# One written order for four engines in a dilated convolution kernel

## The chip, the cores and the metric

The kernel runs on one core of one Trainium2 chip. The metric is the device time of one execution in microseconds. Three runs of the kernel before took 267.48, 267.99 and 269.68 us; their median is 267.99 us. A profile was taken of one further execution.

## The reference

The input x has 2 sequences of 16000 time steps with 256 channels, in bf16. A causal convolution with three taps and dilation 2 gives 512 channels; one half goes through tanh, the other through a sigmoid, their product is multiplied with a 256 x 256 matrix:

```python
B, T, D, K = (2, 16000, 256, 3)
dil = 2
pad = (K - 1) * dil
xp = jnp.pad(x, ((0, 0), (pad, 0), (0, 0)))
h = jnp.einsum('btc,cd->btd', xp[:, pad:pad + T, :], w[0])
for i in range(1, K):
    off = pad - i * dil
    h = h + jnp.einsum('btc,cd->btd', xp[:, off:off + T, :], w[i])
f = h[..., :D].copy()
g = h[..., D:].copy()
z = jnp.tanh(f) * _sigmoid(g)
return z @ w_o
```

## The kernel before

**Groups and blocks.** Time is cut into 26 groups of rows, a row being 4 or 6 successive time steps. A group of kind B (13 of them, 4 steps a row) computes two outputs of each parity from four products where the direct way needs six; a group of kind A (12, 6 steps a row) computes three outputs from five products where the direct way needs nine. One small group P at the very start is done directly. A group has R = 256 rows (160 in the last one and in P), loaded transposed by one DMA on SyncE's queue (line 286). Each A or B group has four blocks, one for every 128 of the 512 channels: 100 blocks in all. The list `seq` holds them in order: four B groups, then A and B blocks mixed, then two B groups.

**What a block needs.** Its products are two matmuls each (two halves of the 256 input channels), 2R columns wide. The letters are those of the code:

- F ("first") starts PSUM bank b. ScalarE copies it to SBUF (c, `copy_first`, line 484), since more is added to b later.
- M ("mid", kind A alone) adds to b. VectorE makes hh from the copy and b (h, `halfway`).
- L ("last") adds to b. VectorE then makes bank a from the copy and b (a) and, for kind A, a third result yy from hh and b (y); both stand in `combine`, and all of h, a and y are recorded at line 487.
- Z ("zero") adds to b, and I ("inf") adds to a. The block's outputs are in b, a and yy.
- ScalarE applies tanh or sigmoid to b, yy and a (b, y, a in its order; line 527). VectorE multiplies tanh and sigmoid halves (g, `gate`, line 547) after the second and the fourth block of a group.
- P: a piece of the last matrix product, four matmuls of 256 columns (`out_mm`, line 565). ScalarE evicts it (e, line 592; the last few go to VectorE at line 576, v), and a store on SyncE's queue follows when all pieces of 128 rows are evicted.

**Input sums.** The moving operands of the products are sums and differences of the loaded rows. VectorE makes most (`pre`, lines 432 and 434). GpSimd makes the operands d0 and d3 of most B groups and r0 and ri of the A groups, in quarters (lines 434). Two more, rm and rp, are made by accumulating DMAs on GpSimd's queue (line 429). GpSimd also adds up the weight matrix of F for the A groups in 16 pieces (wa.0 to wa.15). Each of GpSimd's sums is made to wait (`hold`) for a chosen instruction of VectorE, so that it starts beside one that reads PSUM.

**Slots.** The main loop goes through slots k = 0, 1, ...; in slot k, block k does F (and M), block k-1 does L and its combine, block k-2 does Z and I, and block k-3 has its last activation and its gate. TensorE's order in a slot is fixed by the kinds of the blocks k and k-1:

```python
PE_ORDER = {"AB": "FLZIM12", "AA": "FZLIM12", "BA": "FZLI12", "BB": "FZLI12", "": "LZI123"}
```

The digits are the pieces P, one or two per slot by a rule on the number waiting. ScalarE's order follows from this loop: activation a, one eviction, then copies and activations as their products are issued. On VectorE the gate, then a, y and h follow each other; a written plan (`PLAN`, one line per stop, taken at each gate, each combine and some evictions) tells which input sums VectorE makes before that instruction and which sums GpSimd is given there. Each engine executes its instructions in the order in which the loop issues them; the semaphores between engines are derived from what each one reads and writes.

**Buffers that matter.** Bank b has 3 buffers, so F of block k waits for the activation of b of block k-3. Bank a has 2, the output pieces have 3, the copies 3.

Of the kernel before, what the change touches and what calls it, by code (L numbers as in the profile page):

```python
# [13 lines left out]
PLAN = """  # L14
>m.0 p.0 d3.0 d0.0;
>d3.1;wa.2
>m.1;
>;wa.1
>p.1 d0.2 m.2;wa.5' wa.7
>d0.1;  # L20
>;wa.0
>e.0 u1.0;wa.10
>p.2;
>;wa.8 wa.9
>d3.2 f.0;wa.6' wa.13'
>m.3;
>ud.0;wa.4' wa.12
>uh.0 u0.0 u0.1;r0.0''
>u2.0;
>u3.0;ri.0'  # L30
>u2.1 d0.3;wa.14' wa.3
>d3.3;
>p.3;rp.0 r0.0'
>p.4 f.1;wa.11'
>u0.2;
>u1.1;rm.0 r0.0'
>d0.4 m.4;ri.0' d0.5'
>u1.2;
>d3.4;r0.0'
>ud.1 uh.2 e.1 uh.1;rp.1 r0.2' wa.15  # L40
>;
>u3.1;r0.2' ri.0 ri.0
>m.5 u3.2;d3.5'
>f.2 e.2;rm.1 ri.1' r0.1 r0.1'
>;
>;r0.2 r0.1
>;
>u1.3;ri.1' d0.5'
>u2.2 ud.2;d0.5' r0.1
>;  # L50
>;ri.1 d3.5 ri.1 ri.2 d3.5
>e.3;
>p.5 u3.3 f.3;rm.2 ri.2' d3.5'
>ud.3;
>;rp.2 r0.2
>;
>uh.3;d0.5' d3.6'
>u1.4 u3.4;rp.3 d0.6 d0.6'' ri.2' d3.6''
>u0.3;ri.2
>;  # L60
>u2.3;r0.3' d3.6
>f.4 uh.4;rm.3 ri.3' r0.3''
>;
>u0.4;ri.3' d0.6
>;
>e.4;r0.3' r0.3
>ud.4 m.6;d0.6' r0.4'
>p.6 e.5;ri.3' ri.3''
>;
>;d3.6 r0.4  # L70
>;
>u1.5;rm.4 d3.7'
>u2.4 uh.5 m.7;r0.4' ri.4''
>;
>;rp.4 d3.7 r0.4
>e.6 u3.5 ud.5;ri.4' ri.4
>u0.5 f.5;r0.5' ri.4''
>;
>;r0.5 d3.7
>;  # L80
>u1.6;rp.5 d0.7
>p.7 u2.5;rm.5 d3.7'
>ud.6;
>uh.6;ri.5' r0.5'
>u3.6 u0.6;ri.5' d0.7'
>f.6 u2.6;rm.6 r0.6'' ri.5 r0.5 d0.7
>;
>;ri.5
>;
>f.7;rp.6 d0.7' r0.6'  # L90
>u1.7;ri.6' r0.6'
>u0.7 u2.7;ri.6' ri.6
>;
>u3.7;r0.6' ri.6
>m.8 ud.7 e.7;d0.8' d3.8''
>u1.8;
>;rm.7 d3.8
>;
>;ri.7 d0.8 d0.8 ri.7
>p.8;d0.8'  # L100
>e.8 u3.8 u0.8;rp.7 ri.7' d3.8''
>uh.7;
>;r0.7 d0.9 r0.7 d3.8
>;
>;ri.7
>f.8 u2.8;d3.9' d0.9''
>;
>;r0.7 r0.7
>uh.8 e.9 ud.8;rm.8 ri.8''
>u1.9 uh.9;rp.8 d3.9 ri.8''  # L110
>;
>ud.9;ri.8'
>f.9;
>u3.9;ri.8' r0.8 r0.8
>u2.9;ri.9' r0.8'
>u0.9;d0.9 r0.8
>m.9;
>;d3.9 d3.10
>u1.10;rm.9 r0.9
>;  # L120
>p.9;rp.9 r0.9' d3.9'
>;
>uh.10;d0.9' d0.10'
>f.10 e.10;r0.9 ri.9''
>u3.10 u1.11;d0.10 ri.9''
>;
>;r0.9 ri.9
>;
>u2.10;rm.10 d0.10' d3.10
>u3.11 u0.10 ud.10;rp.10 ri.10'  # L130
>;
>;r0.10 ri.10 r0.10
>ud.11 p.10;r0.10' r0.10''
>e.11 m.10;d3.11' d3.11''
>;
>;ri.10 d3.10 ri.10
>;
>;d0.10 d0.11
>f.11 uh.11 u2.11;rm.11 d3.10 d3.12'
>u0.11;  # L140
>;rp.11 ri.11 r0.11 d3.12 ri.11
>;ri.11 ri.11
>;r0.11 r0.11
>m.11;
>;r0.11 d0.11
>;
>;
>;d3.11 d0.12 d3.12 d0.12
>;d0.12
>;  # L150
>;d0.11
>m.12 p.11;d3.11' d0.11
>;
>;d3.12
>;
>;
>;
>;
>;
p.12>;d0.12  # L160
>;
>;
>;
>;
>;
>;
>;
>;
>;
>;  # L170
>;
>;
# [4 lines left out]
def kernel(  # L177
# [10 lines left out]
    nc = tc.nc  # L188
    bf16 = mybir.dt.bfloat16
    f32 = mybir.dt.float32  # L190
# [15 lines left out]
    SOME, SOME_A = 5, 99  # L206
# [7 lines left out]
    def group(kind, b, t, R):  # L214
        of_kind[kind].append(len(groups))
        groups.append(dict(kind=kind, b=b, t0=t, R=R, J=ROWS[kind]))
        return t + ROWS[kind] * R

    for b in range(B):
        t = 0  # L220
        if b == 0:
            t = group("P", b, 0, 160)
        n_a, n_b = N_A[b], (T - t - 6 * RG * N_A[b]) // (4 * RG)
# [5 lines left out]
        if T > t:  # L229
            t = group("B", b, t, (T - t) // 4)  # L230
# [11 lines left out]
    SHARE = N - 3  # L242
# [254 lines left out]
    def combine(blk):  # L497


        at_stop()  # L500
        g, oi = blk
        G = groups[g]
        n = 2 * G["R"]
        b, ss = G["b", oi][:, :n], G["ss", oi][:, :n]
        G["a", oi] = ps_a.tile([P, 2 * RG], f32, name="a")
        stt(G["a", oi][:, :n], ss, 3.0 if G["kind"] == "A" else -2.0, b)
        if G["kind"] == "A":
            G["y", oi] = ss_pool.tile([P, 2 * RG], f32, name="yy")
            stt(G["y", oi][:, :n], G["hh", oi][:, :n], 2.0, b)
# [23 lines left out]
    def gate(g, dt):  # L533
        at_stop()
# [35 lines left out]
    def out_evict(g, rb0, jp, on_v=False):  # L570
# [3 lines left out]
        if on_v:  # L574
            at_stop()
# [13 lines left out]
        if jp == 0:  # L589
# [3 lines left out]
        if jp == J // 2 - 1:  # L593
# [10 lines left out]
    kinds = {n: groups[g]["kind"] for n, (g, _) in enumerate(seq)}  # L604
    stops = iter([[part.split() for part in re.split("[>;]", line)] for line in PLAN.strip().split("\n")])
    stop = next(stops)
# [68 lines left out]
    gate(0, 0)  # L675
    ahead()
# [5 lines left out]
    final = final[-1:] + final[:-1]  # L682

    todo, made, last_odd = [], [], []
    k = 0
    while k < N + 3 or todo or made:
        b0, b1, b2, b3 = (seq[n] if 0 <= n < N else None for n in (k, k - 1, k - 2, k - 3))
        kind = groups[b0[0]]["kind"] if b0 else None
        n = 1 + (len(todo) >= SOME_A) if kind == "A" else (k >= N + 3) + (not b0 or len(todo) >= SOME) + 1
        pieces = []  # L690
        while todo and todo[0][0] <= k and len(pieces) < n:
            pieces.append(todo.pop(0)[1])

        if b3:
            activate(b3, "a")
        for piece in made[:1]:
            out_evict(*piece)
        for what in PE_ORDER[(kind or "") + (kinds.get(k - 1, "B") if kind else "")]:
            if what == "F":
                product(b0, "first")  # L700
                copy_first(b0)
                if k == 0:
                    direct(3, TAPS[:2], (1,))
                if b2 and groups[b2[0]]["kind"] == "A":
                    activate(b2, "y")
            elif what == "M":
                product(b0, "mid")
            elif what == "L" and b1:
                product(b1, "last")
                if k == 1:  # L710
                    direct(3, TAPS[2:], (1,))
                    activate((0, 3), "a")
            elif what == "Z" and b2:
                product(b2, "zero")
                activate(b2, "b")
                for piece in made[1:] if k < SHARE else ():
                    out_evict(*piece)
            elif what == "I" and b2:
                product(b2, "inf")
            elif what in "123" and len(pieces) >= int(what):  # L720
                if k >= N + 3:
                    out_mm(*pieces[int(what) - 1], dts=(1,))
                elif k >= N and what == "2":
                    out_mm(*pieces[1], pool=ps_b, tag="b")
                else:
                    out_mm(*pieces[int(what) - 1])
        if k == N + 2:

            assert not todo
            for piece, (pool, tag) in zip(final, ((ps_a, "a"), (ps_b, "b"), (ps_o, "o_ps"))):  # L730
                out_mm(*piece, dts=(0,), pool=pool, tag=tag)
        if not b2 and k < SHARE:
            for piece in made[1:]:
                out_evict(*piece)

        if b3 and b3[1] in (1, 3):
            g, dt = b3[0], b3[1] // 2
            gate(g, dt)
            if dt == 1:
                todo += [(k + 1, piece) for piece in (final if g == seq[-1][0] else pieces_of(g))]  # L740
        if k == 0:
            weights_a(1 + K)
        if b1:
            combine(b1)
        if k == 1:
            gate(0, 1)
            todo += [(k + 1, piece) for piece in pieces_of(0)]
        if b0 and kind == "A":
            halfway(b0)
        for n, piece in enumerate(made[1:] if k >= SHARE else ()):  # L750
            out_evict(*piece, on_v=n == 0)
        ahead()
        made = pieces
# [4 lines left out]
        k += 1  # L758

    nc.scalar.dma_start(**last_odd[0])  # L760
# [30 lines left out]
```

## Time and profile before

| | |
|---|---|
| median of the three runs | 267.99 us |
| the profiled execution's own time | 267.66 us |
| its span, first to last instruction | 265.8 us |
| busy: TensorE / ScalarE / VectorE / GpSimd | 259.5 / 245.9 / 240.0 / 144.2 us |
| granted TensorE clock, mean | 0.995 |

Times in the profile are microseconds from the span's start. PE is TensorE's matmuls and PEld its weight loads, DVE is VectorE, ACT is ScalarE, POOL is GpSimd, SP is SyncE. A busy time counts a matmul from its start until its modelled end, which lies after the next one's start, so a short stall can hide in it. In rows of the timeline a trailing x2 means that two instructions of one kind were merged into one row, and a bracket gives the idle time before the row and what ended it. In the chain, each row is a start, a duration and what held the end of the program back at that time.

### The profile page before, as it was taken

How to read it: one execution, taken by the hardware profiler on the slowest of the kernel's cores; microseconds unless marked ns; L12 is line 12 of the kernel's file. 1: busy time of each engine (PE TensorE's matmuls, PEld its weight loads, DVE VectorE, ACT ScalarE, POOL GpSimd, SP SyncE). 2: the span in 40 equal slices, each digit the busy share in tenths (PEclk: the TensorE clock that was granted, in tenths of full speed). 3: DMA queues.
4: the chain of work that ended last, by engine and by line, in shares of the span. 5: the costliest groups of instructions: out<-in, count | busy, mean ns of one | idle time of the engine just before them, and what ended most of it. 6: DMA issues, size and time to landing. Idle time of an engine off the chain costs nothing.

```text
span 265.8 us, 4535 instructions
## 1 busy us (share of the span) xinstructions
PE 259.5 (98%) x1476; PEld 143.0 (54%) x1476; DVE 240.0 (90%) x396; ACT 245.9 (92%) x487; POOL 144.2 (54%) x209
## 2 busy tenths in 40 slices
PE   8999999999999999999999999999999999999993
PEld 4654555554555555555455555555555555555682
DVE  2999999999999999999999999999999996877472
ACT  5889999898999999999999999999999999999983
POOL 1034476677876666466755866476465677423000
PEclk9999999999999999999999999999999999999998
DMA  7999999569394589469729794796139464121225
GB/s 188 224 207 227 229 162 217 149 128 197 66 242 130 121 200 203 120 154 233 178 98 211 174 190 104 184 207 139 61 121 166 123 149 118 61 77 60 101 99 187
DMA packets 79583, 41.25 MB, mean 155 GB/s; under 512 B 68648, under 2 KB 69928, under 8 KB 79560
## 3 DMA queue, kind: packets, MB, share of 16 engines
q1 hardware_dynamic: 75060, 33.66, 52.4%
q0 software_dynamic: 3456, 6.29, 13.8%
q10 hardware_dynamic: 1044, 1.02, 1.2%
q8 instruction: 11, 0.18, 0.3%
q14 instruction: 12, 0.10, 0.1%
HBM read 1.25 MB, written 16.38 MB: 66 GB/s over the span
## 4 chain that ended last, share of the span: by engine, by line
PE 87%; DMA 3%; ACT 3%; DVE 3%; SPq 1%; issue 1%; DVEq 0%
PE b L453 52%; PE o_ps L565 20%; PE a L453 15%; DMA xt<-in_x_dram 2%; DMA w_sb<-in_w_dram 1%; ACT th L527 1%; ACT ss L484 1%; DVE a L487 1%; SPq L286 1%; DVE yy L487 1%; ACT sg L527 1%; DVE hh L487 1%; ACT osb L592 0%; DVE zz L547 0%; DVE p L434 0%
## 5 line engine op out<-in xcount | busy, mean ns | idle before, releaser
L487 DVE SCALAR_TENSOR_TENSOR a<-ss,b 128x512 f32<-128x512 f32 (+1 forms) x100 | 68.4, 684 | 10.3 <-PE b L453 9.3
L592 ACT CAST osb<-o_ps 128x512 bf16<-128x512 f32 x118 | 70.9, 601 | 4.7 <-PE o_ps L565 4.6
L565 PE MATMUL o_ps<-wo_sb,zz 128*128 128x256 bf16 x496 | 69.9, 273 | 0.0
L453 PEld LDWEIGHTS <-w_sb 128*128 128x128 bf16 x400 | 38.8, 97 | 47.2 <-issue 1.9
L484 ACT COPY ss<-b 128x512 f32<-128x512 f32 (+1 forms) x100 | 60.2, 602 | 2.9 <-ACT osb L592 0.8
L565 PEld LDWEIGHTS <-zz 128*128 128x128 bf16 x496 | 48.5, 98 | 25.3
L434 POOL TENSOR_TENSOR d<-xt 128x256 bf16<-128x256 bf16 (+1 forms) x64 | 41.9, 663 | 35.2 <-DVE zz L547 11.3
L434 POOL TENSOR_TENSOR u<-u,uh 128x256 bf16<-128x256 bf16 x48 | 37.6, 789 | 24.9 <-DVE zz L547 17.3
L434 POOL TENSOR_TENSOR u<-u,ud 128x256 bf16<-128x256 bf16 x48 | 36.9, 775 | 24.5 <-DVE zz L547 12.9
L547 DVE TENSOR_TENSOR zz<-th,sg 128x1024 bf16<-128x1024 bf16 (+2 forms) x52 | 41.4, 796 | 2.1 <-ACT sg L527 2.1
L487 DVE SCALAR_TENSOR_TENSOR hh<-ss,b 128x512 f32<-128x512 f32 x48 | 32.9, 684 | 2.7 <-PE b L453 2.2
L487 DVE SCALAR_TENSOR_TENSOR yy<-hh,b 128x512 f32<-128x512 f32 x48 | 32.7, 681 | 0.0
L453 PEld LDWEIGHTS <-wp_sb 128*128 128x128 bf16 x200 | 19.5, 97 | 24.4 <-issue 3.4
L527 ACT ACTIVATE th<-a 128x512 bf16<-128x512 f32 (+1 forms) x50 | 30.7, 614 | 2.0 <-PE a L453 1.0
L527 ACT ACTIVATE sg<-a 128x512 bf16<-128x512 f32 (+1 forms) x50 | 31.0, 619 | 1.5 <-PE a L453 0.4
L527 ACT ACTIVATE th<-b 128x512 bf16<-128x512 f32 (+1 forms) x50 | 30.7, 614 | 0.7 <-PE b L453 0.7
L527 ACT ACTIVATE sg<-b 128x512 bf16<-128x512 f32 (+1 forms) x50 | 30.7, 615 | 0.3 <-PE b L453 0.3
L453 PE MATMUL b<-d,w_sb 128*128 128x512 bf16 (+1 forms) x104 | 30.3, 373 | 0.2 <-DVE a L487 0.2
L453 PE MATMUL a<-d,w_sb 128*128 128x512 bf16 (+1 forms) x104 | 30.3, 373 | 0.0
L453 PE MATMUL b<-m,wm_sb 128*128 128x512 bf16 (+1 forms) x104 | 30.3, 373 | 0.0
L453 PE MATMUL b<-p,wp_sb 128*128 128x512 bf16 (+1 forms) x104 | 30.3, 373 | 0.0
L453 PE MATMUL b<-u,w_sb 128*128 128x512 bf16 x96 | 28.6, 379 | 0.5 <-DVE yy L487 0.3
(57 smaller groups left out, 330.0 us busy)
## 6 DMA issues: line engine op xcount, KB each, us to landing
out_dram<-osb SPq DMA_DIRECT2D x24, 384.0 KB, 2.7
out_dram<-osb SPq DMA_DIRECT2D x26, 256.0 KB, 2.6
f<-u POOLq DMA_DIRECT2D x12, 256.0 KB, 3.9
e<-u POOLq DMA_DIRECT2D x12, 256.0 KB, 3.6
w_sb<-in_w_dram ACTq DMA_DIRECT2D x3, 256.0 KB, 4.0
xt<-in_x_dram SPq DMA_TRANSPOSE x25, 5.4
xn<-in_x_dram SPq DMA_DIRECT2D x1, 160.0 KB
xn<-in_x_dram ACTq DMA_DIRECT2D x1, 160.0 KB, 4.4
```

What stands on the lines that cost most here:

```text
L286: ins = nc.sync.dma_start_transpose(out=xt[:, :, :, RH - lo:RH + R].rearrange("p j ct r -> p (j ct) r"), in_=x[G["b"], G["t0"] - J * lo:G[ ...
L434: ins = eng.tensor_tensor(out=o, in0=a, in1=b, op=op)
L453: nc.tensor.matmul(G[bank, oi][:, :2 * R], lhsT=wmat[:, ct, osl], rhs=G[mv][:, :, ct, :R], start=which == "first" and ct == 0, stop=ct == ...
L484: nc.scalar.copy(out=G["ss", oi][:, :n], in_=G["b", oi][:, :n])
L487: return note(nc.vector.scalar_tensor_tensor(out=out, in0=in0, scalar=scalar, in1=in1, op0=ALU.mult, op1=op))
L527: nc.scalar.activation(out=G[name, dt][:, j:j + 2, :R], in_=G[bank, oi][:, :2 * R].rearrange("p (q r) -> p q r", q=2), func=(ACT.Tanh, ACT ...
L547: note(nc.vector.tensor_tensor(out=G["z"][:, dt, :, :n], in0=G["th", dt][:, :, :n], in1=G["sg", dt][:, :, :n], op=ALU.mult))
L565: nc.tensor.matmul(o_ps[:, q, :], lhsT=z, rhs=wo_sb[:, dt, :], start=dt == 0 and (q == 0 or len(dts) == NT), stop=dt == NT - 1, skip_group ...
L592: copy(out=osb[:, 2 * jp:2 * jp + 2, :], in_=o_ps[:])
```

## The change

The plan has one line for each slot now, 106 lines with k = -1 first, and each line has four parts: TensorE's products and pieces in their order, ScalarE's activations, copies and evictions in theirs, VectorE's sums, gates, combines, halfways and evictions in theirs, and GpSimd's sums. The fixed table of orders, the rule on the number of pieces and the stops are gone. `combine` is split, so that a and y can stand apart (y may come before a). The instructions are the same in number and kind on each engine; which groups there are, how they load, and how far ahead, stays as it was. In code, the parts of a line are issued so that ScalarE's next letter goes out as soon as what it reads has been issued. GpSimd's sums are given out ahead of a in each slot.

```diff
 PLAN = """
->m.0 p.0 d3.0 d0.0;
->d3.1;wa.2
->m.1;
...
->f.2 e.2;rm.1 ri.1' r0.1 r0.1'
->;
->;r0.2 r0.1
...
+ |  | d3.0 m.0 p.0 d0.0 G | 
+F D D | c w |  | 
+F L D | c d | d3.1 a m.1 G | wa.7' wa.4
+F L Z I | c b | a | wa.1 wa.5
+L P F Z I | a c b | d0.2 a | wa.2
+L Z P F I | a b c | m.2 p.1 g a | wa.9
...
+F L I Z M P P | c a y b | e.2 a u3.1 h | ri.1' d0.5'
+F Z L I M | a e e c b | g f.2 a h y | rm.1 r0.1' r0.1 r0.2'
+F P I L Z P | a e c e y b | g u1.3 a y | ri.1' r0.2 ri.1'
+L F I Z M | a c y b | a u2.2 h | d0.5
+Z F L I M | a e c b | g a y h | r0.1 r0.2
...
+Z I P p P | a b | v | 
+H H H | a e E | g v | 
+R R R |  |  | 
+ | e E | v | 
 """
...
-    def combine(blk):
-
-
-        at_stop()
+    def combine(blk, what):
...
-        G["a", oi] = ps_a.tile([P, 2 * RG], f32, name="a")
-        stt(G["a", oi][:, :n], ss, 3.0 if G["kind"] == "A" else -2.0, b)
-        if G["kind"] == "A":
+        if what == "a":
+            G["a", oi] = ps_a.tile([P, 2 * RG], f32, name="a")
+            stt(G["a", oi][:, :n], ss, 3.0 if G["kind"] == "A" else -2.0, b)
+        else:
             G["y", oi] = ss_pool.tile([P, 2 * RG], f32, name="yy")
             stt(G["y", oi][:, :n], G["hh", oi][:, :n], 2.0, b)
...
-    def ahead():
-        sums(stop[0])
-        stop[0] = []
-
-    def at_stop():
-        nonlocal stop
-        sums(stop[1])
-        gpsimd(stop[2])
-        stop = next(stops, [[], [], []])
...
-    PE_ORDER = {"AB": "FLZIM12", "AA": "FZLIM12", "BA": "FZLI12", "BB": "FZLI12", "": "LZI123"}
...
-        n = 1 + (len(todo) >= SOME_A) if kind == "A" else (k >= N + 3) + (not b0 or len(todo) >= SOME) + 1
...
+    for k, line in enumerate(PLAN.strip().split("\n"), -1):
+        pe, act, dve, pool = (part.split() for part in line.split("|"))
         b0, b1, b2, b3 = (seq[n] if 0 <= n < N else None for n in (k, k - 1, k - 2, k - 3))
...
+        def scalar():
+
+            while waiting:
+                what = waiting[0]
+                there = {"c": "F" in done, "b": "Z" in done, "e": made, "E": made[1:], "d": not leftover}
+                if not there.get(what, True):
+                    break
+                waiting.pop(0)
+                if what == "c":
+                    copy_first(b0)
+                elif what in "by":
+                    activate(b2, what)
+                elif what == "a":
+                    activate(b3, "a")
...
+        scalar()
+        for what in pe:
+            if what in "FM":
+                product(b0, {"F": "first", "M": "mid"}[what])
+            elif what == "L":
                 product(b1, "last")
...
+            done.add(what)
+            scalar()
...
+        for what in dve:
+            if what == "g":
+                gate(b3[0], b3[1] // 2)
...
+            elif what == "a":
+                gpsimd(pool)
+                combine(b1, "a")
+            elif what == "y":
+                combine(b1, "y")
+            elif what == "h":
+                halfway(b0)
+            elif what == "v":
+                out_evict(*made.pop(0), on_v=True)
+            else:
+                sums((what,))
```

More of the change, by code (lines that the diff above doesn't have):

```diff
@@ new lines @@
+F I Z L P P | a y b c | y a g | r0.11
+F L I Z M | a c e y b | a h g | d3.11 d3.11 d3.11
+Z P F I L M | b c a e e | p.11 a h y | d3.12'
+F P P P I L Z P P | a e e c y b | m.11 a y | d3.11'
+L F I Z M | a y c b e | m.12 a h g | d0.11
+I Z F L P | a b c e | a y | d3.12 d0.11
+F L I Z | a c y b e | a g |
+L Z I F P | b a e c | p.12 a g | d0.12 d3.12
+F P P Z L I P | a e c e b e | a | d3.12 d0.12
+L I Z F P P | a b c | a g |
+F L I Z P P | a e e c b | a v | d0.12
+L F Z P I | a c b e | a g v |
+L Z I P F P | a e b c | a |
@@ L228 @@
                 t = group("A", b, t, RG)
-        if T > t:
-            t = group("B", b, t, (T - t) // 4)
+        rows = (T - t) // 4
+        while rows:
+            t = group("B", b, t, 160 if rows % P else P)
+            rows = (T - t) // 4
     As, Bs = of_kind["A"], of_kind["B"]
@@ L674 @@
     next(wb)
-    gate(0, 0)
-    ahead()
-    PE_ORDER = {"AB": "FLZIM12", "AA": "FZLIM12", "BA": "FZLI12", "BB": "FZLI12", "": "LZI123"}
     final = pieces_of(seq[-1][0])
-    final = final[-1:] + final[:-1]
+    if final[-1][2] is None:
+        final = final[-1:] + final[:-1]
+    firsts = iter(zip(final, ((ps_a, "a"), (ps_b, "b"), (ps_o, "o_ps"))))
+    seconds = iter(final)
+    leftover = list(TAPS)
     todo, made, last_odd = [], [], []
-    k = 0
-    while k < N + 3 or todo or made:
+    for k, line in enumerate(PLAN.strip().split("\n"), -1):
+        pe, act, dve, pool = (part.split() for part in line.split("|"))
@@ L687 @@
         b0, b1, b2, b3 = (seq[n] if 0 <= n < N else None for n in (k, k - 1, k - 2, k - 3))
-        kind = groups[b0[0]]["kind"] if b0 else None
-        n = 1 + (len(todo) >= SOME_A) if kind == "A" else (k >= N + 3) + (not b0 or len(todo) >= SOME) + 1
[L690 to L708, printed above, removed]
-                product(b1, "last")
[L710 to L753, printed above, removed]
+        if ">" in dve:
+            sums(dve[:dve.index(">")])
+            dve = dve[dve.index(">") + 1:]
@@ new lines @@
+        waiting, done = list(act), set()
+        def scalar():
[11 more added lines that the diff above has]
+                    activate(b3, "a")
+                elif what == "d":
+                    activate((0, 3), "a")
+                elif what == "w":
+                    weights_a(1 + K)
+                else:
+                    out_evict(*made.pop("eE".index(what)))
@@ new lines @@
+        scalar()
[3 more added lines that the diff above has]
+            elif what == "L":
+                product(b1, "last")
+            elif what in "ZI":
+                product(b2, {"Z": "zero", "I": "inf"}[what])
+            elif what == "D":
+                direct(3, (leftover.pop(0),), (1,))
+            elif what == "H":
+                piece, (bank, tag) = next(firsts)
+                out_mm(*piece, dts=(0,), pool=bank, tag=tag)
+            elif what == "R":
+                made.append(next(seconds))
+                out_mm(*made[-1], dts=(1,))
+            else:
+                made.append(todo.pop(0))
+                out_mm(*made[-1], **({"pool": ps_b, "tag": "b"} if what == "p" else {}))
+            done.add(what)
+            scalar()
@@ new lines @@
+        assert not waiting, (k, waiting)
+        for what in dve:
+            if what == "g":
+                gate(b3[0], b3[1] // 2)
+                if b3[1] == 3 and b3 != seq[-1]:
+                    todo += pieces_of(b3[0])
+            elif what == "G":
+                gate(0, int(k > 0))
+                if k > 0:
+                    todo += pieces_of(0)
+            elif what == "a":
[7 more added lines that the diff above has]
+                out_evict(*made.pop(0), on_v=True)
+            else:
+                sums((what,))
@@ L757 @@
             loaded += 1
-        k += 1
-    nc.scalar.dma_start(**last_odd[0])
+    assert not todo and not made
+    for store in last_odd:
+        nc.scalar.dma_start(**store)
 _INS = ['x', 'w', 'w_o']
```

247 lines of the change are left out of this document (83 added, 164 removed).

## The prediction

> **What bounds the kernel now.** The first page gives the busy shares and the chain by engine:
>
> ```profile
> span 265.8 us, 4535 instructions
> PE 259.5 (98%) x1476; PEld 143.0 (54%) x1476; DVE 240.0 (90%) x396; ACT 245.9 (92%) x487; POOL 144.2 (54%) x209
> ...
> PE 87%; DMA 3%; ACT 3%; DVE 3%; SPq 1%; issue 1%; DVEq 0%
> ```
>
> TensorE is the bound, and the change neither adds nor takes away an instruction of it. So the only thing to win is time in which TensorE stands still, and 98% hides how much that is. The chain in order of time shows it; each row is a start, a duration and a count of matmuls:
>
> ```profile
> 105.64 0.44 PE o_ps L565 x4
> 106.08 1.34 PE b L453 x6
> 107.42 0.43 PE a L453 x2
> 107.85 0.87 PE o_ps L565 x8
> 108.72 1.30 PE b L453 x6
> ```
>
> Six matmuls into b take 1.30 in one slot and 1.34 in another: three products of 0.433 each, and 0.04 of standing still in the second, which a busy time doesn't show because the previous matmul's modelled end covers it. A matmul of 512 columns takes 0.373 but the next starts 0.2165 after it (a row "x2" lasts 0.59); one of 256 columns 0.109 after it (the row of 0.87 for 8); one of 320 columns 0.135. From the start of slot 2 (13.09) to the last matmul's end (261.27) the trace has 858 x 0.2165 + 32 x 0.135 + 496 x 0.109 = 244.1 us of such steps. The stretch is 248.2, of which 0.2 is the last matmul's drain: **about 4 us of standing still.** Going through the timeline, the gaps over 0.025 add up to 4.0, in four classes:
>
> - Z waits for a of a B block: 0.39 (13.91) and 0.13 (30.50), 0.52.
> - Z waits for yy of an A block: 0.25 (65.68), 0.43 (127.64), 0.28 (241.31), 0.03, together 0.99.
> - L waits for hh of an A block: 18 times, mostly 0.04 to 0.05, together 1.26.
> - F waits for ScalarE's activation of bank b: 12 times, 0.03 to 0.28, together 1.24.
>
> What is outside (11 us of head, 4.5 us from the last matmul to the span's end, and 1.8 between span and execution time) the change leaves alone.
>
> **Why these gaps, and what the new order does to each.** I count, for each wait, the TensorE pieces (0.433 each) that the written order puts between a release and the wait for it, and compare with what the chain on the other engine needs.
>
> *The hh chain.* The timeline of slots 40 and 41:
>
> ```profile
> 104.18 0.59 PE L453 MATMUL b<-f,wp_sb 128*128 128x512 bf16 x2
> 104.90 0.69 DVE L487 SCALAR_TENSOR_TENSOR a<-ss,b 128x512 f32<-128x512 f32 x1
> 105.50 0.68 DVE L487 SCALAR_TENSOR_TENSOR yy<-hh,b 128x512 f32<-128x512 f32 x1
> 106.09 0.68 DVE L487 SCALAR_TENSOR_TENSOR hh<-ss,b 128x512 f32<-128x512 f32 x1
> 106.35 0.59 PE L453 MATMUL b<-u,w_sb 128*128 128x512 bf16 x2
> 106.83 0.59 PE L453 MATMUL b<-f,wp_sb 128*128 128x512 bf16 x2
> ```
>
> L of one block ends at 104.77; a, yy, hh run one after the other; the next block's L starts 0.06 after hh's end. From the moment TensorE could go on after the first L (104.61) to hh's release it is 0.16 of drain, 0.04 to 0.13 until a starts, 0.60, 0.59, 0.68 and 0.06: 2.13 to 2.22. The fixed order "FZLIM" with a piece, then "FZL", puts five pieces there, 2.165. So the margin is nothing, at each of the 19 places where an A block follows an A block (once there are four pieces, 1.73). In the new plan the chain a, y, h stands against five pieces in one place (slot 18); everywhere else there are at least 0.2 to spare. Of 1.26 I keep 0.05.
>
> *The yy chain* needs, by the same rows without hh, 1.53 to 1.62; before, two A blocks had three pieces (1.30: gaps 0.25 and 0.28). The new plan never has fewer than four (1.73). The gap of 0.43 at 127.64 had four and another cause, a VectorE sum held up beside a GpSimd sum:
>
> ```profile
> 124.87 0.98 POOL L434 TENSOR_TENSOR u<-u,uh 128x256 bf16<-128x256 bf16 x1
> 125.23 1.16 DVE L434 TENSOR_TENSOR u<-xt 128x1024 bf16<-128x1024 bf16 x1
> ```
>
> That sum takes 0.69 elsewhere; the rest delays a, yy and Z. Such meetings aren't excluded after: I keep 0.40 of the 0.99.
>
> *Z after a* needs 0.16 + 0.04 + 0.69 + 0.06 = 0.95; four B blocks had two pieces and the first one less. The new plan has at least three (1.30).
>
> ```profile
> 12.56 0.70 DVE L434 TENSOR_TENSOR d<-xt 128x1024 bf16<-128x1024 bf16 x1 [0.33 <-DMA xt<-in_x_dram]
> 13.09 0.59 PE L453 MATMUL b<-m,wm_sb 128*128 128x512 bf16 x2
> 13.17 0.69 DVE L487 SCALAR_TENSOR_TENSOR a<-ss,b 128x512 f32<-128x512 f32 x1
> 13.91 0.38 PE L453 MATMUL b<-d,w_sb 128*128 128x512 bf16 x1 [0.23 <-DVE a L487]
> ```
>
> Here a load lands at 12.54, d3 follows, then a, and Z starts at 13.91 although F was over by 13.52. In the new line (F L Z I) the next L fills just that time. Then VectorE is late itself: in slots 3 and 4 it has d0.2 (its load lands at 16.12 in both), a, m.2, p.1, a gate, a, which by 0.60 each ends at about 19.89, while Z could start at 19.66. With 0.07 in the slot before, 0.30 stays of 0.52. The first d3 now goes ahead of m; m then ends at 10.55 instead of 9.95, and TensorE is busy with the first group until 10.97.
>
> *F after ScalarE.* Drain 0.16, start 0.04, activation 0.61, release 0.06: 0.87, just two pieces (0.866), if ScalarE is free at that instant. The old order left two pieces four times and paid 0.16, 0.09, 0.28 and nothing (mean 0.13); the new one leaves two pieces 28 times for F, and 13 times for M behind the copy (0.60: 0.86 needed). These **41 tight places** are where the new order saves its room from. Bounds for one: below, nothing, as the need equals the room, and ScalarE's order now puts this instruction where its product ends; above, 0.28, the row at 62.84, where a third instruction stood ahead of it. I take 0.025, much nearer to nothing, since the new plan moves evictions behind the activation in those slots: 1.0 in all (0 to 11.5).
>
> *Moved and hidden.* The pieces P of the first group come one to two slots later and their evictions up to three; the loads ahead of them on SyncE's queue (issued at 4.55 to 21.73) don't wait for these. The accumulating DMA with the least lead, rp of the last A group, goes out in slot 85 for an L in slot 87: 16 pieces, 6.9 us, against 0.87 of issue and 3.9 to landing. GpSimd finishes 15 operands only in the slot before their use, in both plans; TensorE waited for none of them before. At the end, between the last I and the final matmuls there are the same six items in both plans, and no gap before; nothing changes.
>
> **The sum.** Left over: 0.05 + 0.40 + 0.30 + 1.0 = 1.75 of 4.0, a gain of 2.25 us. The profiled execution took 267.66, so 265.4; it lies 0.33 below the median of the runs, 267.99, so I predict 265.8 for the median (265.74). A change of under 1% (2.7 us) is what a measurement of this kernel can hardly tell from none: 265.3 to 270.7.
>
> **Rivals.**
>
> *Nearly all gaps go.* If the 41 places cost nothing and no meeting of the two engines reaches Z, 0.35 to 1.3 is left: a gain of 2.7 to 3.65, 264.3 to 265.3. For it: all chains on VectorE have room now. Against: ScalarE is at 92% and can't always be free in time.
>
> *VectorE and GpSimd meet more often.* Slots in which GpSimd is given more sums than VectorE has instructions reading PSUM rise from 15 to 22, the surplus must run beside sums that read SBUF. One meeting cost 1.16 - 0.69 = 0.47; with 0.2 spare before Z, 0.27 gets through. Twelve more of them are 3.2 us, left 4.95: 268.9, or with half as many 267.3, no change. The Trainium skill (SBUF — State Buffer, "Who interferes with whom") speaks for this one: it has VectorE and GpSimd take a shared port as an exclusive lock, so that a VectorE instruction with two SBUF inputs waits out a GpSimd one that reads SBUF. The row at 125.23 agrees: the sum ended 0.54 after GpSimd's, not much less than its usual 0.69.
>
> *ScalarE becomes the bound: slower.* The order saves room at 41 places where the need equals it. Should ScalarE run late by the mean of before (0.13), they cost 5.5, left 6.2: 270.2; at 0.2 each 8.2, left 8.95, 272.9. It decides from (4.0 - 0.75) / 41 = 0.08 per place on. For it: three of the four tight places before did stall. Against: there the copy of the next block stood right ahead of the activation.
>
> *The plan doesn't set the order.* If the letters didn't come out as the engines' order, the gaps would stay: 268.0.
>
> **The numbers.** The main case, gain 1.3 to 2.7 (265.3 to 266.7), 0.40; nearly all gaps go, 0.28; meetings, 267 to 269, 0.16; ScalarE late, 269 to 273, 0.12; no effect, 0.04. Under 265.3 falls the second case and a little of the first, 0.30; over 270.7 most of the fourth, 0.10; between, 0.60. The range leaves out the lowest 0.06 and about 0.14 above: 264.5 to 269.0.
>
> **What would show it.** In the chain, rows of 1.34 to 1.43 for six matmuls into b become 1.30; hh vanishes as a releaser of TensorE; Z at the head follows at about 13.96 without a gap. Wrong would be: gaps of 0.1 and more before F or M behind an activation or a copy (ScalarE), VectorE sums over 0.9 followed by a gap before Z, or GpSimd as TensorE's releaser.

## The result and the profile after

The change made the kernel a little slower. Nine runs after have a median of 269.48 us (268.64 to 270.22), nine runs before beside them 267.81 us (267.48 to 269.68). The ratio is 1.0058, with a 95% interval of 1.0036 to 1.008. The prediction was 265.8, and its range ended at 269.0. The profiled execution after took 268.89 us, 1.23 more than the one before. Two single executions are left out of every ratio because they ran far slower: 971.83 us of the new order without GpSimd's sums (0.84 us from one matmul of 512 columns to the next instead of 0.2165, and no row of the granted clock in the trace), and 436.61 us of the kernel before (granted clock 0.589).

The first page of the kernel after, the same three lines as before:

```profile
span 267.1 us, 4517 instructions
...
PE 259.2 (97%) x1476; PEld 143.5 (54%) x1476; DVE 243.6 (91%) x396; ACT 244.7 (92%) x487; POOL 145.9 (55%) x209
...
PE 74%; DVE 22%; issue 2%; ACT 1%; DVEq 0%
```

Instructions of each engine are the same in number. VectorE is busy for 3.6 us longer with the same 396 instructions (240.0 before), and its share of the chain went from 3% to 22%. So instructions of VectorE take longer, and TensorE waits for them.

I counted TensorE's standing still as in the prediction: each start-to-start step against 0.2165, 0.135 or 0.109 us by columns, gaps over 0.025 added up. Beside it stands how much longer VectorE's instructions took than the median of their own kind (over 0.06 each), called **hold-ups** from here on.

| | before | after |
|---|---|---|
| gaps of TensorE, sum (count) | 3.99 (36) | 4.85 (23) |
| released by a | 0.52 | 3.21 |
| released by yy | 0.99 | 0.67 |
| released by hh | 1.25 | 0.69 |
| released by ScalarE | 1.23 | 0.27 |
| VectorE's hold-ups, sum (count) | 2.32 (14) | 6.17 (13) |
| the longest hold-up | 0.47 | 1.88 |
| TensorE's last matmul ends at | 261.27 | 262.52 |
| from there to the span's end | 4.56 | 4.57 |

The regular gaps did go: hh no longer stops TensorE in 18 places, and ScalarE hardly at all. In their place a few large gaps have come, and three quarters of all the time that TensorE stands still follows four hold-ups. The largest is in slots 39 to 41. The timeline of the kernel after, where each row is start, duration, engine, line, operation, output and inputs:

```profile
103.46 0.88 POOL L377 DMA_DIRECT2D f<-u  x1
...
104.07 1.48 POOL L382 TENSOR_TENSOR d<-xt 128x256 bf16<-128x256 bf16 x2
104.16 2.30 DVE L380 TENSOR_SCALAR ud<-u 128x1024 bf16<-128x1024 bf16 x1
...
105.22 0.95 POOL L382 TENSOR_TENSOR u<-u,ud 128x256 bf16<-128x256 bf16 x1
...
106.38 0.41 DVE L380 TENSOR_SCALAR uh<-u 128x1024 bf16<-128x1024 bf16 x1
...
106.72 0.95 DVE L494 TENSOR_TENSOR zz<-th,sg 128x1536 bf16<-128x1536 bf16 x1
...
107.58 0.68 DVE L435 SCALAR_TENSOR_TENSOR a<-ss,b 128x512 f32<-128x512 f32 x1
...
108.32 0.59 PE L401 MATMUL a<-u,w_sb 128*128 128x512 bf16 x2 [1.36 <-DVE a L435]
```

ud is a scaling that takes 0.41 us, like uh below it. Here it takes 2.30: it starts while GpSimd is issuing the accumulating DMA for rp, and ends only after the three sums queued behind that DMA. uh, the gate and a are late by that, and I stands still for 1.53 (108.32). The chain of the kernel after, in order of time (start, duration, what held the end back), shows the same stretch:

```profile
105.64 0.45 PE b L401 x2
106.09 0.23 PE a L401
106.32 0.06 issue
106.38 0.41 DVE uh L380
106.80 0.87 DVE zz L494
107.66 0.62 DVE a L435
108.28 0.04 issue
108.32 0.59 PE a L401 x2
108.91 0.59 PE b L401 x2
```

The last two rows show what follows: two matmuls take 0.59 instead of 0.433 from start to start, since yy and hh come right behind a, 0.60 apart, and TensorE waits 0.16 more for each. With those gaps (108.91, 109.51, 111.91) the one hold-up cost 2.0 us. The other three are a sum of 1.60 at 38.36 instead of 0.69 (gap 0.71 at 40.62), a gate of 1.46 at 89.06 instead of 0.95 (gap 0.30 at 91.17) and a sum of 1.37 at 134.61 instead of 0.69 (gap 0.56 at 137.24). A gate at 75.35, 0.36 too long, gives 0.25 at 78.32. Together these five make 3.84 of the 4.85 us.

### The profile page after: what moved, and what is told of

It reads as the page before. It is cut to its first block, busy times and chain, and to the rows that moved or that the text cites. A ratio compares the mean times of both kernels' runs of the same rounds, so it can differ in the third digit from the quotient of the medians.

```text
span 267.1 us, 4517 instructions
## 1 busy us (share of the span) xinstructions
PE 259.2 (97%) x1476; PEld 143.5 (54%) x1476; DVE 243.6 (91%) x396; ACT 244.7 (92%) x487; POOL 145.9 (55%) x209
## 2 busy tenths in 40 slices
DMA packets 79583, 41.25 MB, mean 154 GB/s; under 512 B 68648, under 2 KB 69928, under 8 KB 79560
## 3 DMA queue, kind: packets, MB, share of 16 engines
HBM read 1.25 MB, written 16.38 MB: 66 GB/s over the span
## 4 chain that ended last, share of the span: by engine, by line
PE 74%; DVE 22%; issue 2%; ACT 1%; DVEq 0%
PE b L401 41%; PE o_ps L512 16%; PE a L401 12%; DVE a L435 5%; DVE zz L494 4%; DVE hh L435 3%; DVE yy L435 3%; DVE u L382 2%; PE b L421 1%; PE a L421 1%; DVE f L382 1%; PE a L216 1%; DVE uh L380 1%; DVE p L382 0%; DVE d L382 0%
## 5 line engine op out<-in xcount | busy, mean ns | idle before, releaser
L537 ACT CAST osb<-o_ps 128x512 bf16<-128x512 f32 x118 | 69.6, 622 | 0.4 <-PE o_ps L512 0.2
L382 POOL TENSOR_TENSOR d<-xt 128x256 bf16<-128x256 bf16 (+1 forms) x64 | 44.1, 705 | 28.6 <-DVE zz L494 13.8
L382 POOL TENSOR_TENSOR u<-u,ud 128x256 bf16<-128x256 bf16 x48 | 38.9, 814 | 23.6 <-DVE zz L494 10.3
L401 PE MATMUL a<-u,w_sb 128*128 128x512 bf16 x96 | 28.5, 379 | 1.8 <-DVE a L435 1.8
```

The source lines that it names most:

```text
L382: ins = eng.tensor_tensor(out=o, in0=a, in1=b, op=op)
L401: nc.tensor.matmul(G[bank, oi][:, :2 * R], lhsT=wmat[:, ct, osl], rhs=G[mv][:, :, ct, :R], start=which == "first" and ct == 0, stop=ct == ...
```

## The experiments

The theory after the result: **the written order does remove the regular gaps, but GpSimd's sums now run where VectorE has instructions that both engines can't do at once, and what these lose is more than what was won.** The rivals: the new order itself is no better (ScalarE or TensorE's order); the early launches (a sum held behind an earlier instruction of VectorE than the last one, written with a ' in the plan) cause the meetings; or any placing of GpSimd's sums costs that much.

### GpSimd's sums taken away, in the new order and in the old

Both kernels leave GpSimd's sums out; a memset writes to the same tile at the same place.

```diff
-        return nc.gpsimd.tensor_tensor(out=dst[:, d], in0=wu_sb[0][ct][:, d], in1=wu_sb[1 + add][ct][:, d], op=ALU.add)
+        return nc.gpsimd.memset(dst[:, d], 0.0)
...
-        if op is None:
+        if eng is nc.gpsimd:
+            ins = eng.memset(o, 0.0)
+        elif op is None:
```

> The new order, with every sum that GpSimd makes replaced by GpSimd writing a constant to the same place, behind the same wait; these sums are left out of the computation. Theory (VectorE's input sums are held up by GpSimd's sums, 6.2 us of excess in the trace, and TensorE stands still behind them): the long VectorE sums go, TensorE's standing still falls from 5.0 to about 1 us, 264 to 265.5 us. Rival (the new VectorE order itself is too tight): stays above 267.5.

> The old order with the same replacement; the sums of GpSimd are left out of the computation. Theory: 2.3 us of excess go from VectorE, but the gaps that five pieces against a, yy, hh leave stay: 266 to 267 us, so the new order is 1.5 to 2.5 us better than the old where GpSimd makes no sums. Rival (the order saves nothing on the chip): both without sums within 0.7 us of each other.

The new order without the sums took 265.56 us, ratio 0.9917 (0.990 to 0.9933) to the kernel before; the old order without them 267.73, ratio 0.9997 (0.9982 to 1.0012), more than the 266 to 267 that was expected. So the new order by itself is worth 2.1 us (0.9997 - 0.9917, of 268). GpSimd's sums cost the new order 3.8 us (1.0058 - 0.9917) and the old one nothing that can be measured. The trace of the new order without the sums is from one further execution:

> The new order with GpSimd's sums replaced by constants (left out of the computation), once more for a trace, since its one profiled execution ran with the TensorE clock far down. Theory: about 265.5 us; the excess of VectorE's sums 0; TensorE's standing still under 1.5 us, none of it over 0.3 in one place.

It took 266.74 us, 1.2 more than the median above. The first page of the new order without GpSimd's sums:

```profile
span 265.0 us, 4507 instructions
...
PE 258.7 (98%) x1476; PEld 143.9 (54%) x1476; DVE 238.2 (90%) x396; ACT 244.0 (92%) x487; POOL 71.1 (27%) x209
...
PE 97%; DVE 1%; ACT 0%; issue 0%
```

VectorE has no hold-up at all here, and 5.4 us less of busy time than after. The gaps are 1.91 us, of which 1.15 (0.90 at 19.30 and 0.25 at 21.71) follow a load that lands late (at 17.93, where it landed at 15.94 in the kernel after); under 1.5 in all, and none over 0.3 in one place, were expected. This execution also began its first group 0.8 us later than the one after. In the old order without the sums VectorE has no hold-up either, and the regular gaps stay: 1.18 from ScalarE, 1.03 from hh. So GpSimd's sums delay instructions of VectorE, and the memsets don't. A memset only writes to SBUF, and it is shorter (0.31 us for 0.67); the runs don't show which of the two it is. The delay goes the other way too: the 12 memsets that start during one of VectorE's scalings take 0.42 to 0.53 us.

### The sums in the old plan's slots

The new order for TensorE, ScalarE and VectorE, with each of GpSimd's entries in the slot that the old plan gave it (12 of the 200 had to come later).

```diff
-F Z I L | a c b | e.0 u1.0 d0.1 a | wa.6' wa.0'
+F Z I L | a c b | e.0 u1.0 d0.1 a | wa.10
-L P F Z I | a e e c b | a d3.2 p.2 g | wa.3
+L P F Z I | a e e c b | a d3.2 p.2 g | wa.8 wa.9
...
```

> The new order of TensorE, ScalarE and VectorE; GpSimd's sums are given out in the slots (and behind the same number of instructions) of the old plan, 12 of 200 a little later since what they read is made later. Theory in its narrow form (the new placement of GpSimd's sums is what meets VectorE's): excess of VectorE back to 2 to 3 us, 265.5 to 267.5 us. Rival (any placement that isn't made for this VectorE order meets its sums): 268.5 to 270.5, excess of VectorE 5 us or more.

It took 271.29 us, ratio 1.0134 (1.0109 to 1.0159): worse than the change, and beyond both expected ranges. VectorE's hold-ups rose to 9.4 us in 37 places, and GpSimd became a releaser of TensorE, which it never was before or after. From the waits (us in total, times, longest):

```profile
PE a L401 <- POOL u L382: 1.1, 2, 0.8
```

So the old slots weren't better in themselves. The sums and the order of VectorE around them have to be placed together; taking one from one plan and the other from another is worse than either.

### No early launches

Every ' is taken out, so each sum waits for the last instruction of VectorE ahead of a.

```diff
-F L D | c d | d3.1 a m.1 G | wa.7' wa.4
+F L D | c d | d3.1 a m.1 G | wa.7 wa.4
...
-F Z I L | a c b | e.0 u1.0 d0.1 a | wa.6' wa.0'
+F Z I L | a c b | e.0 u1.0 d0.1 a | wa.6 wa.0
...
```

> The new order with every sum of GpSimd held behind the last VectorE instruction ahead of a, none earlier. If sums that were let go early are what meets VectorE's input sums: 266 to 268 us. If the meetings come from sums that queue up behind each other on GpSimd (three in a row beside one VectorE sum of 2.30 us): no gain, 269 to 271, with more surplus sums running late.

It took 269.23 us, ratio 1.0053 (1.0036 to 1.007), the same as the change; the hold-ups are 6.7 us in 33 places. The large one is there again, on the other scaling. The timeline of this kernel:

```profile
104.33 1.09 POOL L377 DMA_DIRECT2D f<-u  x1
...
104.94 1.68 POOL L382 TENSOR_TENSOR d<-xt 128x256 bf16<-128x256 bf16 x2
...
105.25 2.29 DVE L380 TENSOR_SCALAR uh<-u 128x1024 bf16<-128x1024 bf16 x1
```

The early launches are not what makes the loss: without them it is as large. What the two kernels share is a DMA issue with three sums behind it, in a slot where VectorE has only two instructions that read PSUM (a and h).

### Four sums moved

Slots 38 and 39 have seven sums and two DMA issues for GpSimd, and four instructions of VectorE that read PSUM. Four of the sums go to slots 40 and 48, which had none:

```diff
-F Z I L P P | a y b c e | p.6 g m.7 a y | rm.4 d0.7' r0.4 d3.6 d3.6'
-F P L M Z I P | c a y e b | u2.4 a h | rp.4 d3.7 d0.7' ri.4'
-Z F L P M I | a c b e e | ud.5 uh.5 g a y h | 
+F Z I L P P | a y b c e | p.6 g m.7 a y | rm.4 d3.6 d3.6'
+F P L M Z I P | c a y e b | u2.4 a h | rp.4 ri.4'
+Z F L P M I | a c b e e | ud.5 uh.5 g a y h | d0.7 d3.7 r0.4
...
-F L Z P M I | a e e c e b e | u2.6 a y h | 
+F L Z P M I | a e e c e b e | u2.6 a y h | d0.7
```

> The new plan with four of GpSimd's 200 sums given out later: in slots 38 and 39 d0.7 (twice), d3.7 and r0.4 go, three of them to the empty slot 40 and one to slot 48; nothing needs them before slot 44. Theory: the VectorE sum of 2.30 us at 104.2 and the 1.11 us one at 101.9 go, with them the gaps of 1.53, 0.16, 0.17 and 0.16 at slots 41 and 42: 1.8 to 2.0 us less than the changed kernel, 267.3 to 267.8. Rival (VectorE is simply behind its plan there): the gap stays, 269.0 or more.

It took 267.34 us, ratio 0.997 (0.9953 to 0.9987), which is 2.4 us (0.0088 of 268) less than the change. The timeline of this kernel, at the same place:

```profile
102.68 0.86 POOL L377 DMA_DIRECT2D f<-u  x1
...
103.37 0.87 POOL L382 TENSOR_TENSOR u<-u,ud 128x256 bf16<-128x256 bf16 x1
...
104.39 0.41 DVE L380 TENSOR_SCALAR ud<-u 128x1024 bf16<-128x1024 bf16 x1
...
105.99 0.69 DVE L435 SCALAR_TENSOR_TENSOR a<-ss,b 128x512 f32<-128x512 f32 x1
...
106.15 1.18 POOL L382 TENSOR_TENSOR d<-xt 128x256 bf16<-128x256 bf16 x2 [1.91 <-DVE zz L494]
```

One sum is left behind the DMA issue; it is over by 104.24, ud takes its 0.41, and the gaps of 1.53, 0.16, 0.17 and 0.16 are gone. The others of the change stand as they were (0.75 at 41.25, 0.56 at 135.77, 0.30 at 91.81). One crowded slot was worth more than what the whole change lost against before.

### The other crowded slots

In a first step 13 sums move to a later slot (the four among them), in a second 15, some of them others (20 lines of the plan differ from the change, in GpSimd's part alone). Some of the lines:

```diff
-L P Z F I | a e e b c | m.4 u1.2 a p.4 g | rm.0 ri.0''
+L P Z F I | a e e b c | m.4 u1.2 a p.4 g | rm.0
...
-L F P P Z M I | c a b y e | u1.4 a h g | d3.5' d0.5' d3.6
+L F P P Z M I | c a b y e | u1.4 a h g | d3.5' d0.5'
...
-F P L Z M I | a e c b y e | g a h | d0.6
+F P L Z M I | a e c b y e | g a h | d0.6 d3.6
```

> The same and ten more of GpSimd's sums given out elsewhere, each because a VectorE sum was held up beside it (slots 14, 20, 23, 28, 33, 47, 50). Theory: of the 4.85 us of standing still 1.0 to 1.8 are left: 265.6 to 266.6, faster than the old kernel by 0.5 to 0.9%. Rival (the meetings only move to other places, as GpSimd has no more room beside instructions that read PSUM): 267.5 or more with an excess of 4 us or more.

> As the kernel with fourteen sums moved, with d0.5, d0.6, r0.2, ri.2 and ri.3 placed anew, since that kernel's trace has five of GpSimd's sums in a row at 67.2 to 70.9 and a gap of 0.42 at 74.1 behind them, and a gate of 1.46 us at 81.2. Theory: 0.4 to 0.6 us less than that kernel, 265.7 to 266.2. Rival (the rest is due to loads that land late and to short waits): 266.2 to 266.8.

The first took 266.38 us, ratio 0.992 (0.9895 to 0.9945), with 2.5 us of hold-ups; the second **265.72 us** (265.62 to 266.71, beside 267.99), ratio 0.9918 (0.9902 to 0.9934). The second beats both kernels, and its ratio is that of the new order without GpSimd's sums (0.9917). Its first page:

```profile
span 264.1 us, 4516 instructions
...
PE 258.2 (98%) x1476; PEld 143.4 (54%) x1476; DVE 239.6 (91%) x396; ACT 244.1 (92%) x487; POOL 143.9 (54%) x209
...
PE 91%; DMA 4%; SPq 2%; DVE 1%; issue 0%; ACT 0%; DVEq 0%
```

TensorE's gaps are 1.89 us, 0.68 of them (0.43 at 18.09, 0.25 at 20.50) after a load of the head. VectorE's hold-ups are 2.0 us, none over 0.33. So the sums can be placed at next to no cost, in the order of the change.

### What one meeting costs

A kernel of its own, which computes nothing of the reference. ScalarE releases both engines at once; VectorE first does a short instruction reading PSUM and then the one that is timed, which so arrives 0.16 us after GpSimd's first of n sums (128 x 256) has started.

```diff
+    for kind in ("tt", "ts", "psum"):
+        for n in (0, 1, 2, 3, 4):
+            for rep in range(4):
+                last = trial(kind, n, last)
```

> A kernel of its own that computes nothing of the reference: ScalarE releases GpSimd and VectorE together; GpSimd makes 0 to 4 sums of 128x256 back to back, VectorE a short instruction on PSUM and then one of three: a sum of two SBUF tiles (128x1024), a product of one SBUF tile with a number (128x1024), an instruction that reads SBUF and PSUM (128x512). Theory (GpSimd keeps the port through all that it has queued, as the 2.30 us instruction beside three sums suggests): the first two grow with every sum, by about 0.6 us each, to 2 us and more over their 0.69 and 0.42 at four; the third stays at 0.68. Rival (VectorE waits for the sum in progress alone): no more than 0.6 us over, however many are queued, and GpSimd's second sum is late instead.

| VectorE's instruction | n = 0 | n = 1 | n = 2 | n = 3 | n = 4 |
|---|---|---|---|---|---|
| sum of two tiles in SBUF | 0.685 | 1.055 | 1.055 | 1.055 | 1.055 |
| scaling of one tile in SBUF | 0.420 | 0.790 | 0.790 | 0.790 | 0.790 |
| with one input in PSUM | 0.681 | 0.681 | 0.681 | 0.681 | 0.681 |

The timeline of this kernel, with four sums of GpSimd merged into one row:

```profile
41.27 2.99 POOL L44 TENSOR_TENSOR pz<-px,py 128x256 bf16<-128x256 bf16 x4 [0.51 <-ACT trig L41]
41.43 1.05 DVE L51 TENSOR_TENSOR dz<-da,db 128x1024 bf16<-128x1024 bf16 x1
```

VectorE waits for the sum that is running and no further: 0.37 at this offset, whatever stands behind it. GpSimd's second sum then waits in its turn (1.115 instead of 0.667 beside a sum, 0.848 beside a scaling). So sums in a row alone can't explain 2.30, and the theory that the wait grows with each of them fell. The Trainium skill (SBUF — State Buffer, "Who interferes with whom") has a shared pair of ports that one of the two engines holds for a whole instruction, and lets an instruction of VectorE with one input in SBUF, outside the two-port modes, go free. The table's first and last rows agree. The scaling has one input in SBUF as well and is held up, so by that rule it would be in a two-port mode, which no run here shows.

### The same behind a DMA issue

The same, with an accumulating DMA (128 x 1024) issued by GpSimd ahead of its n sums. The issue's row runs from 0.29 to 1.17 us after the release, the sums follow; VectorE's instruction arrives before the issue, early in it, or near its end.

```diff
+        sent = hold(nc.gpsimd.dma_start(out=fa[:], in_=ua[:], accum_op=ALU.add), [go])
+        ends = [sent]
...
+                for ahead in ((128,), (512,), (512, 256)):
```

> A kernel of its own that computes nothing of the reference, as the one before it, but GpSimd first issues an accumulating DMA of 128x1024 and then makes 0, 1 or 3 sums back to back, and the VectorE instruction under test (128x1024, two SBUF inputs or one) arrives 0.24, 0.63 or 1.0 us after the release. Theory (the issue of such a DMA ahead of a sum is what makes VectorE wait for more than one of GpSimd's instructions): with three sums some arrival waits 1.5 us or more, with the DMA alone 0.3 or more. Rival (VectorE waits for one sum at most here too): no wait over 1.0 us, none for the DMA alone.

| arrives after the release at | n = 0 | n = 1 | n = 3 |
|---|---|---|---|
| sum: 0.24, before the issue | 0.685 | 0.685 | 0.685 |
| sum: 0.64, early in the issue | 0.685 | 1.795 | 3.03 |
| sum: 1.09, near its end | 0.685 | 1.34 | 2.57 |
| scaling: 0.64 | 0.47 | 1.53 | 2.77 |
| scaling: 1.09 | 0.42 | 1.07 | 2.31 |

The timeline of this kernel, one trial with three sums:

```profile
91.80 0.88 POOL L43 DMA_DIRECT2D fa<-ua  x1 [1.28 <-ACT trig L42]
92.14 3.03 DVE L55 TENSOR_TENSOR dz<-da,db 128x1024 bf16<-128x1024 bf16 x1
92.41 2.21 POOL L46 TENSOR_TENSOR pz<-px,py 128x256 bf16<-128x256 bf16 x3
```

The three rows repeat those at 103.46 to 105.22 of the kernel after. VectorE's instruction arrives in the issue, and ends 0.55 after the last of three sums; each further sum costs it 0.62, while without the DMA it cost nothing. The issue alone (n = 0) costs 0.05 at most, where 0.3 was expected. So a DMA issue by itself doesn't keep VectorE out, but in these trials VectorE loses the turn between the sums behind it. The instruction that arrives later only ends at the same time (0.64 + 3.03 and 1.09 + 2.57).

The rows hold a hint. The sums behind the issue start 0.625 apart, as they do without the DMA, but each lasts 0.95, so that the next has started 0.33 before the last one ends; without the DMA the two overlap by 0.04. Spans on GpSimd are rough, so this doesn't show the mechanism.

Nor does every instruction that arrives in an issue wait. In the timeline of the kernel after, a scaling takes its usual 0.41 in the very issue that holds up the sum behind it:

```profile
133.63 1.14 POOL L377 DMA_DIRECT2D f<-u  x1
...
134.24 1.18 POOL L382 TENSOR_TENSOR d<-xt 128x256 bf16<-128x256 bf16 x1
134.28 0.41 DVE L380 TENSOR_SCALAR u<-u 128x1024 bf16<-128x1024 bf16 x1
134.61 1.37 DVE L382 TENSOR_TENSOR u<-xt 128x1024 bf16<-128x1024 bf16 x1
```

What decides between the two stays open.

### The DMA issues behind the sums

If the order of issue and sums is the cause, the issues may go last. In the plan of the change, rm and rp are put behind the sums of their slot, in 21 slots:

```diff
-F Z I L P P | a y b c e | p.6 g m.7 a y | rm.4 d0.7' r0.4 d3.6 d3.6'
+F Z I L P P | a y b c e | p.6 g m.7 a y | d0.7' r0.4 d3.6 d3.6' rm.4
```

> The new plan with the accumulating DMAs (rm, rp) issued after GpSimd's sums of the same slot instead of ahead of them, in 21 slots; nothing else is changed. Theory (in the trace four of the five largest hold-ups, 0.69 to 1.88 us, have such an issue just ahead of the sum): the excess of VectorE falls from 6.2 to 3 to 4 us and the time to 267.0 to 268.3. Rival (GpSimd is late by the number of sums alone): 269 or more.

It took 279.95 us, ratio 1.0454 (1.0413 to 1.0495). The expectation was wrong for a reason that it hadn't counted: a sum waits for an instruction of VectorE, and an issue behind it waits with it, so the DMAs land too late. From the waits of this kernel:

```profile
PE b L401 <- DMA e<-u: 5.8, 3, 3.5
PE b L401 <- DMA f<-u: 1.7, 1, 1.7
```

And the hold-ups stay (7.0 us): the sums of the next slot now stand behind the issue. (The expectation counts four of the five largest hold-ups of the kernel after behind an issue; its trace has three, 1.88, 0.92 and 0.69.) That edit is no remedy, and its time says nothing for or against the cause. Its longest hold-up does say something: VectorE needn't arrive during the issue. In the timeline of this kernel the issue is over at 132.13, a sum of VectorE starts at 132.51, and it ends 0.56 after the last of the four sums behind that issue:

```profile
131.26 0.87 POOL L377 DMA_DIRECT2D f<-u  x1
...
131.88 2.20 POOL L382 TENSOR_TENSOR u<-u,ud 128x256 bf16<-128x256 bf16 x3
...
132.51 2.69 DVE L382 TENSOR_TENSOR u<-xt 128x1024 bf16<-128x1024 bf16 x1
...
133.76 0.88 POOL L382 TENSOR_TENSOR d<-xt 128x256 bf16<-128x256 bf16 x1
```

## Why the prediction was wrong, step by step

**What bounds the kernel: right.** TensorE's instructions took the same time; the gaps and the start tell the result. The last matmul ended 1.25 later: 0.86 more of gaps, 0.23 from a later first F (11.20 for 10.97), the rest in steps under 0.025. One count in the prediction is off: 500 matmuls of 256 columns, not 496, which makes the steps 0.44 us longer. The 4.0 us of gaps were added up one by one and don't rest on it.

**The hh chain: right.** The 18 regular gaps are gone; 0.08 is left of hh in the new order without GpSimd's sums, where 0.05 was kept. Of the 0.69 after, 0.62 are in the wake of late VectorE work; the other 0.08 (75.49) is that same place.

**The yy chain: its own part was right** (0.09 left without the sums), the 0.40 kept for meetings was not; see below.

**Z after a, at the head: right.** In the timeline of the kernel after, the next L fills the time and Z follows without a gap, at 14.18 where about 13.96 was said, as TensorE's first group began 0.23 later:

```profile
13.31 0.70 DVE L435 SCALAR_TENSOR_TENSOR a<-ss,b 128x512 f32<-128x512 f32 x1 [0.21 <-PE b L401]
...
13.74 0.59 PE L401 MATMUL b<-p,wp_sb 128*128 128x512 bf16 x2
...
14.18 0.59 PE L401 MATMUL b<-d,w_sb 128*128 128x512 bf16 x2
```

The 0.30 kept for the second place of the head didn't come in this execution, where the load landed at 15.94, not at 16.12. It came, larger, in others: 1.15 and 0.68 us above. That this term hangs on when a load lands was seen, but not that it moves by that much from run to run.

**F after ScalarE, the 41 tight places: mis-sized.** 1.0 was kept; all gaps released by ScalarE are 0.27 us after, and 0.55 in the new order without GpSimd's sums. One such place in the timeline of the kernel after: the activation that frees F's bank runs from 112.54 to 113.14, and F starts at 113.21, right behind the two matmuls that began at 112.77 (0.433 later):

```profile
112.54 0.60 ACT L475 ACTIVATE sg<-b 128x512 bf16<-128x512 f32 x1
...
112.77 0.59 PE L401 MATMUL b<-d,w_sb 128*128 128x512 bf16 x2
...
113.21 0.59 PE L401 MATMUL b<-u,wa_sb 128*128 128x512 bf16 x2
```

So the bound from below, nothing, was nearly the value, and the rival in which ScalarE becomes the bound falls: 0.01 for each place in both, far from its 0.08.

**Moved and hidden: right**, for what happened: the tail is the same to 0.01 us, no operand of GpSimd and no DMA was late. The kernel with the issues behind the sums shows how near that edge is.

**The step that failed: the 0.40 kept for meetings of VectorE and GpSimd.** They cost 3.84 us, nearly ten times that. Without this term the sum came near: 0.05, 0.30 and 1.0 left, a gain of 2.65, against 2.2 measured with the sums away (1 - 0.9917, of 268). That they lie so close is partly luck: in the trace without the sums a at the head leaves 1.18 where 0.30 was kept, ScalarE 0.55 where 1.0 was. The rival that named this mechanism gave 268.9 for twelve further meetings at a price of 0.47; 269.48 came out. But it wasn't more meetings that did it, as the rival said: there are 13 hold-ups after and 14 before. They are longer, 0.47 on average instead of 0.17, with one of 1.88. I priced the meeting by the largest row of before, 0.47 at 125.23, as the price of any meeting. That row was itself behind a DMA issue on GpSimd's queue, which the two lines in the prediction leave out. From the timeline of the kernel before:

```profile
124.23 0.87 POOL L429 DMA_DIRECT2D e<-u  x1
```

Only one sum (124.87) stood behind that issue, and it was the only hold-up of this sort before, so the row couldn't show that the wait grows with the number of sums. After, in three of the 13 VectorE arrives during such an issue, with one, three and one sum behind it (38.36, 104.16 and 134.61), and these three hold 3.49 of the 6.17 us. The letters of the plan could have told part of that: slot 39 has rp.4 ahead of three sums, and two instructions reading PSUM. I counted surplus slots, 15 against 22, and didn't ask which of them had a DMA issue, nor by how much a slot was over. The count was also the wrong sign to go by: of the three issues with a hold-up behind them only the one of slot 39 is in a surplus slot; those of slots 14 and 50 have one sum each. A sign of being wrong that the prediction named did come, sums of VectorE over 0.9 followed by a gap (38.36 and 134.61), but the largest hold-up was a scaling.

**The chances** gave this rival 0.16. The count of surplus slots spoke for it, and the working brought nothing against it. The 0.40 was carried over from before, where one hold-up reached TensorE; but the old order without GpSimd's sums was no faster (0.9997), so that small cost belonged to the old placing of the sums and said nothing of the new.

## What to carry to other kernels

Where two engines share a way into memory, a new order of one of them is not priced until the other's work has been laid beside it, instruction by instruction: take the second engine's work out in both orders first, and it is clear what the order is worth (2.1 us here) and what the meetings take (3.8). Look at the few longest instructions against the median of their kind, not at how many there are. A crowded stretch is mended by moving a few instructions of the engine that has time to spare, and here four of GpSimd's 160 input sums were worth 2.4 us.

## What the runs showed of the hardware that was not expected

Behind a DMA issued from GpSimd's queue, VectorE doesn't get its turn between GpSimd's sums. In the trials a sum of VectorE that arrives during the issue takes 3.03 us with three sums behind it, 1.795 with one, against 1.055 without the DMA; in the kernel with the issues last, a sum that arrives 0.38 after the issue has ended takes 2.69. The rule of the Trainium skill (SBUF — State Buffer, "Who interferes with whom") cited above, of a pair of ports held for one instruction, doesn't by itself give this. The runs don't show what keeps VectorE out in between, nor why some instructions pass (0.41 at 134.28). GpSimd's sums start 0.625 apart there as without the DMA, but their rows last 0.95 to 0.97 us instead of 0.667. An issue without sums behind it costs VectorE nothing to 0.05 us in the trials, and 0.08 at 195.81 of the kernel after.
